# Attention scores as plain fp32 products on the two row halves of TensorE, with one maximum per unit

## The chip, the cores and the metric

The kernel runs on one core of a Trainium2 chip. The metric is device time in microseconds from the start to the end of one execution. The engines are TensorE (PE, with its weight loads shown as PEld), VectorE (DVE), ScalarE (ACT), GpSimd (POOL) and SyncE (SP), which issues the transfers.

## The reference

Attention over 4 batches and 8 heads, 576 tokens, 64 values per head, is mixed with a read of a memory and followed by two stacks of matrix products. Only the first part is touched by the change:

```python
scores = scale * np.matmul(q, k.transpose(0, 1, 3, 2))     # scale = 1/8
scores = np.where(causal, -1000000000.0, scores)
scores = scores - scores.max(-1, keepdims=True)
a = np.exp(scores)
a /= a.sum(-1, keepdims=True) + 1e-09
local = np.matmul(a, v)
...
attn = g * mem_out + (1 - g) * local
x = attn over tokens, 2304 x 512
h = (x @ w1) * (x @ w2) @ w3 ;  x = h @ w_out
h = x @ w_in ;  out = (h - tanh(h)) @ w_out2
```

All arrays are fp32, and the weights of the two stacks arrive as 64-bit numbers that the kernel decodes itself.

## The kernel before

**Stages.** The first stage, from the start to about 302 us, is the attention. In its gaps it decodes `w3` and `w_out`, multiplies them with each other (tiles `fo`, `zs`, `wf`), decodes the first tiles of `w1` and `w2` and reads the memory for the first 384 tokens. Then come the product with `w1` and `w2` and the folded weight (tiles `ab` and `x`), and from about 655 us the last stack (`h` and `o`).

**Units.** The attention works on 16 pairs of heads P. The queries of a pair are cut into five units u: units 0 to 3 have 128 queries of each head and look at 128(u+1) keys, and unit 4 has the last 64 queries of both heads together, on the two halves of the partitions, and looks at all 576 keys. That makes 80 units, which pass through seven steps in a fixed order, `ORDER = "SENTLGA"` with the lags in `LAG`: S (`scores`, then `rmax`), E (`exps`), N (`norm`), T (`trans`), L (preparation of the next pair), G (some steps of background work, `BG` per unit, from the generator `early`) and A (`av`, the product with v). A scheduler that knows only the dependences then fixes the order on each engine.

**Preparation (`load_qk`, `prep_qk`).** `load_qk` fetches q and k of a pair, transposed, with each 64-row head twice, on partitions 0 to 63 and again on 64 to 127, in two transfers of 576 KB (L196; for the first pair six smaller ones). The pool `r` has `RB` = 2 buffers. `prep_qk` makes reduced-precision parts that TensorE multiplies in one pass: ACT writes the scaled high part of q (L219), DVE overwrites partitions 64 to 127 with the low part (L224), ACT and POOL write the high part of k (`ks`, L204 and L208), and DVE and POOL the low part (L226). The 128 rows of the array thus hold the high and the low part of one head's q.

**Scores and softmax.** `scores` makes two PSUM tiles `sc` of one bank per unit from u = 2 on, one for each head (for unit 4 one for each part of the keys, 320 and 256), and one tile for both heads where they fit in a bank (u < `U1` = 2). Each head takes two matmuls, with the high and the low part of k, and one with the mask (`identb`, `maskb`). The pool of `sc` has `SB` = 4 banks. `rmax` takes the maximum on DVE (L391 for both heads at once in units 0 and 1; L394 once for each tile, with L397 joining the two of unit 4). `exps` runs on ACT, one instruction for each tile, with the sum read out after it (L407). `norm` adds 1e-9 and inverts on DVE (L416, L418, L420) and scales on POOL (L427). `trans` turns the result with TensorE (tiles `t`, L459 to L470) and copies it to `g` on ACT or DVE (`copy`). `av` multiplies v and `g` as plain fp32, the two heads on the two halves of the array's columns, into tiles `o`. The memory read (`mem_mm`, tiles `mo`) also uses plain fp32, in 64 x 64 quarters of the array.

```python
for y in range(2):                     # before: S, for each tile
    scores(n, y)
    rmax(n, y)
```

## Time and profile before

| | |
|---|---|
| median of 3 runs | 1062.58 us (1062.35 to 1063.51) |
| the profiled execution's own time | 1063.58 us |
| its span in the trace | 1061.8 us |
| PE busy in the span | 986.8 us, 93% |
| DVE busy in the span | 816.0 us, 77% |
| ACT busy in the span | 614.4 us, 58% |
| POOL busy in the span | 423.4 us, 40% |

The span runs from the first to the last instruction of the trace; the profiled execution's own time is 1.8 us longer, which lies around the span. A share of busy time is an average over stages with different limits, so it is read stage by stage. A matmul's record reaches to its modelled end, after the next one has begun, so records overlap. An fp32 product appears as two MATMUL records, an fp32r product as one. "f32" in a shape stands for both types where the operand is read by TensorE.

### The profile page before, as it was taken

Reading aid. Unit: us, or ns where it says so; the run is one execution under the profiler, and the core shown is the slowest. Engines: PE = TensorE matmul, PEld = TensorE weight load, DVE = VectorE, ACT = ScalarE, POOL = GpSimd, SP = SyncE. Lnnn points to the kernel's source line nnn. Section 1 sums busy time; section 2 is a strip of 40 time slices with the busy share of each in tenths; the row PEclk is TensorE's granted clock in tenths of the full one; section 3 lists DMA queues with packets and bytes.
Section 4 is the critical chain, followed back from the end, with each engine's and each line's share of the span. In section 5 each row is a group of like instructions: output and inputs, shape, how many; then the busy total and the mean of one; then the engine's idle time right before and its main releaser. Section 6 shows DMA issues by size and latency. Waiting matters only on the chain.

```text
span 1061.8 us, 15818 instructions
## 1 busy us (share of the span) xinstructions
PE 986.8 (93%) x5512; PEld 862.6 (81%) x5512; DVE 816.0 (77%) x1473; ACT 614.4 (58%) x1419; POOL 423.4 (40%) x432
## 2 busy tenths in 40 slices
PE   5799898978998898999999997999999999999998
PEld 3576666655687787999999997989999999999997
DVE  7989998999869998558221288788778788787776
ACT  5567677666732443334121444877777776776764
POOL 5888777777656422200000185322222222222221
PEclk9699999999999898999999999999999999999999
DMA  9764675552324454215000010000000000000000
GB/s 248 190 168 118 176 197 131 135 134 85 95 71 143 142 181 149 60 52 168 30 1 1 1 61 1 1 1 30 1 1 30 1 31 1 2 30 1 31 1 30
DMA packets 44415, 77.73 MB, mean 73 GB/s; under 512 B 5168, under 2 KB 30000, under 8 KB 42416
## 3 DMA queue, kind: packets, MB, share of 16 engines
q1 hardware_dynamic: 44336, 76.73, 25.7%
q8 instruction: 43, 0.70, 0.3%
q14 instruction: 36, 0.29, 0.1%
HBM read 72.00 MB, written 4.72 MB: 72 GB/s over the span
## 4 chain that ended last, share of the span: by engine, by line
PE 66%; DVE 21%; issue 4%; POOL 4%; ACT 2%; DMA 2%; SPq 0%; DVEq 0%; POOLq 0%; ACTq 0%
PE o L143 21%; PE h L143 19%; PE ab L143 13%; PE x L143 7%; DVE T L81 3%; DVE T L75 2%; PE sc L143 2%; POOL p L427 2%; DVE st L394 2%; DVE T L84 2%; PE fo L143 2%; DVE qs L224 2%; DVE T L77 2%; PE t L459 1%; DVE ks L226 1%
## 5 line engine op out<-in xcount | busy, mean ns | idle before, releaser
L925 POOL TENSOR_TENSOR gl<-s,gh 128x384 fp32r<-128x384 f32 x96 | 100.6, 1048 | 292.5 <-ACT gh L919 281.8
L427 POOL TENSOR_SCALAR p<-p,st 128x128 f32<-128x128 f32 (+2 forms) x144 | 111.7, 787 | 55.1 <-DVE st L420 25.8
L143 PE MATMUL x<-abh,wf 128*128 128x384 f32 x384 | 110.5, 349 | 4.1 <-ACT abh L726 4.1
L143 PE MATMUL ab<-xh,wa 128*128 128x384 f32 x384 | 110.3, 345 | 4.0 <-DVE a L723 2.0
L143 PE MATMUL ab<-xh,wb 128*128 128x384 f32 x384 | 108.4, 340 | 2.9 <-POOL wb L96 2.0
L143 PE MATMUL sc<-ks,qs 128*128 128x256 f32 (+4 forms) x384 | 91.7, 358 | 18.5 <-DVE qs L224 9.5
L407 ACT ACTIVATE p<-sc,st 128x256 f32<-128x256 f32 (+4 forms) x160 | 82.5, 527 | 32.6 <-DVE st L394 13.3
L901 DVE SCALAR_TENSOR_TENSOR s<-s,u 128x384 f32<-128x384 f32 x96 | 82.0, 855 | 22.0 <-ACT s L891 21.0
L723 DVE TENSOR_TENSOR a<-ab,a 128x384 f32<-128x384 f32 x48 | 26.4, 551 | 85.8 <-PE ab L143 73.0
L74 ACT ACTIVATE T<-raw 128x512 f32<-128x512 f32 x72 | 48.7, 677 | 67.8 <-POOL wa L99 14.0
L897 ACT ACTIVATE u<-u,pc 128x384 f32<-128x384 f32 x96 | 59.3, 619 | 43.6 <-DVE s L901 43.5
L143 PEld LDWEIGHTS sc<-ks,qs 128*128 128x128 f32 x384 | 63.0, 205 | 26.1 <-ACT p L407 10.1
L907 DVE TENSOR_TENSOR t<-h,t 128x384 f32<-128x384 f32 x96 | 53.3, 555 | 38.1 <-ACT t L890 37.7
L143 PEld LDWEIGHTS ab<-xh,wa 128*128 128x128 f32 x384 | 71.2, 191 | 8.8 <-issue 3.2
L143 PEld LDWEIGHTS x<-abh,wf 128*128 128x128 f32 x384 | 72.8, 195 | 5.3 <-ACT abh L726 5.0
L459 PE MATMUL t<-ident,p 128*128 128x128 f32 x320 | 54.7, 292 | 22.4 <-DVE g L440 8.1
L889 ACT ACTIVATE u<-h 128x384 f32<-128x384 f32 x96 | 47.0, 490 | 47.2 <-PE h L143 47.2
L143 PEld LDWEIGHTS ab<-xh,wb 128*128 128x128 f32 x384 | 71.2, 191 | 3.9 <-POOL wb L96 2.3
L143 PE MATMUL x<-abl,wf 128*128 128x384 f32 x192 | 67.9, 354 | 4.2 <-DVE abl L727 4.2
L906 DVE SCALAR_TENSOR_TENSOR s<-s,s 128x384 f32<-128x384 f32 x96 | 61.3, 638 | 8.5 <-DVE s L901 0.9
L143 PE MATMUL ab<-xl,wa 128*128 128x384 f32 x192 | 65.6, 341 | 0.0
L913 DVE COPY_PREDICATED s<-u,t 128x384 f32<-128x384 uint32 x96 | 58.5, 610 | 8.6 <-ACT t L890 0.5
(228 smaller groups left out, 2796.6 us busy)
## 6 DMA issues: line engine op xcount, KB each, us to landing
r<-in_qk SPq DMA_DIRECT2D x30, 576.0 KB, 7.4
raw<-in_wo SPq DMA_DIRECT2D x24, 512.0 KB, 3.6
raw<-in_w3t SPq DMA_DIRECT2D x16, 512.0 KB, 4.8
raw<-in_w SPq DMA_DIRECT2D x16, 512.0 KB, 3.6
raw<-in_wi SPq DMA_DIRECT2D x16, 512.0 KB, 3.8
v<-in_vt SPq DMA_DIRECT2D x16, 320.0 KB, 6.6
mw<-in_qt SPq DMA_DIRECT2D x18, 256.0 KB, 3.1
out<-ob SPq DMA_DIRECT2D x18, 256.0 KB, 2.3
```

What stands on the lines that cost most here:

```text
L74: AC.activation(out=tf, in_=hw.bitcast(F32), func=AF.Abs)
L143: return PE.matmul(o, lhsT, rhs, start=start, stop=stop).ins
L407: mark["A"][n] = AC.activation(out=p_t[n][:, o:o + w], in_=sc_t.pop((n, x))[:, 0:w], func=AF.Exp, bias=st[:, b:b + 1], accum_out=st[:, 2 + ...
L427: (DV if NV[u] == "V" else PO).tensor_scalar(out=pr, in0=pr, scalar1=sc, scalar2=1.0, op0=ALU.mult, op1=ALU.mult)
L459: PE.transpose(t[:, m], p[:, K * h + 128 * kb:K * h + 128 * kb + 128], ident)
L889: AC.activation(out=u, in_=o, func=AF.Square)
L897: AC.activation(out=u, in_=u, func=AF.Relu, bias=pc[:, 2:3])
L901: DV.scalar_tensor_tensor(out=s1, in0=s1, scalar=k2[0], in1=u, op0=ALU.add, op1=ALU.mult)
L906: DV.scalar_tensor_tensor(out=s1, in0=s2, scalar=k2[1], in1=s1, op0=ALU.add, op1=ALU.mult)
L907: DV.tensor_tensor(out=t, in0=o, in1=t, op=ALU.subtract)
L913: DV.copy_predicated(out=s1, mask=u[:].bitcast(U32), data=t)
L925: PO.tensor_tensor(out=l, in0=s1, in1=h[:].bitcast(F32), op=ALU.subtract)
```

## The change

q and k are fetched once, the first head of the pair on partitions 0 to 63 and the second on 64 to 127, in one transfer of 576 KB per pair in place of two, into one of three buffers. No parts are made; ACT scales q in place (`scale_q`), at the step L of unit 2 of the pair before. The scores are plain fp32 products with 64 rows: head 0 on the upper row half of the array, head 1 on the lower, each into its own bank of a two-bank tile. Unit 4 uses the four 64 x 64 quarters and cuts the keys into 288 and 288. `rmax` is one instruction per unit, over both banks, and unit 4 has one exponential of 576 columns instead of two. The pool of `sc` has two tiles of two banks in place of four of one. The masks, `norm` but for the sum of unit 4, `trans`, `av`, the background work and everything after the attention stay.

```diff
-    PB, RB = 5, 2
+    PB, RB = 5, 3
-    SB = 4
+    SB = 2
     def load_qk(P):
-        r = apr.tile([128, 4, 576], F32, tag="r", name="r")
-        for c in ((slice(1, 3), slice(0, 1), slice(3, 4)) if P == 0 else (slice(0, 4),)):
-            for x in (0, 64):
-                SP.dma_start(out=r[x:x + 64, c], in_=qk[P].rearrange("p (a n) -> p a n", a=4)[:, c])
+        r = qk_t[P] = apr.tile([128, 2, 576], F32, tag="r", name="r")
+        for c in (slice(0, 128), slice(128, 576)) if P == 0 else (slice(0, 576),):
+            SP.dma_start(out=r[:, :, c], in_=qk[P].rearrange("p (a n) -> p a n", a=2)[:, :, c])
-    def prep_qk(P):
...
+    def scale_q(P):
+        for c in (slice(0, 128), slice(128, 576)) if P == 0 else (slice(0, 576),):
+            q = qk_t[P][:, 0, c]
+            AC.activation(out=q, in_=q, func=AF.Copy, scale=0.125)
+        def scores(n):
             P, u = units[n]
+            q, k = qk_t[P][:, 0], qk_t[P][:, 1]
+            hr = [(h, slice(64 * h, 64 * h + 64)) for h in range(2)]
+            sc = sc_t[n] = pss.tile([128, 2, 512], F32, tag="sc", name="sc")
+            if u < 4:
+                K = 128 * (u + 1)
+                for h, r in hr:
+                    mm(sc[:, h, 0:K], q[r, 128 * u:128 * u + 128], k[r, 0:K], True, False)
+                for h, r in hr:
+                    mm(sc[:, h, K - 128:K], identb, maskb[:, 0:128], False, True)
             else:
+                for x in range(2):
+                    for h, r in hr:
+                        y = x ^ h
+                        mm(sc[r, y, 0:288], q[r, 512:576], k[r, 288 * y:288 * y + 288], True, y == 0)
+                mm(sc[:, 1, 224:288], identb, maskb[:, 128:192], False, True)
-            mark["V"][n] = DV.tensor_reduce(out=st_t[n][:, x:x + 1], in_=sc_t[n, x][:, 0:width(u, x)], axis=AX.X,
-                                            op=ALU.max, negate=True).ins
-            if u == 4 and x == 1:
-                DV.tensor_tensor(out=st_t[n][:, 0:1], in0=st_t[n][:, 0:1], in1=st_t[n][:, 1:2], op=ALU.min)
+            mark["V"][n] = DV.tensor_reduce(out=st[:, 0:2] if u < 4 else st[:, 0:1], in_=seen(n),
+                                            axis=AX.X if u < 4 else AX.XY, op=ALU.max, negate=True).ins
-            else:
-                DV.scalar_tensor_tensor(out=st[:, 4:5], in0=st[:, 2:3], scalar=1e-9, in1=st[:, 3:4],
-                                        op0=ALU.add, op1=ALU.add)
+            DV.tensor_scalar(out=st[:, 4:4 + w], in0=st[:, 2:2 + w], scalar1=1e-9, scalar2=None, op0=ALU.add)
             elif x == "L":
+                if u == 0 and 1 <= P <= 16 - RB:
+                    load_qk(P + RB - 1)
+                if u == 2 and P < 15:
+                    scale_q(P + 1)
```

The order on TensorE changes as follows. Before, in a pair in the middle of the folding (units 2 and 3; `sc` are the scores, `t` the transposes, `o` the product with v), the scores of the two heads were separate groups, with other work between them:

```order
L143 MATMUL sc<-ks_106,qs_104 128x384 x2
L143 LDWEIGHTS identb
L143 MATMUL sc<-maskb,identb 128x128
L143 MATMUL sc<-ks_106,qs_104 128x512 x2
L143 LDWEIGHTS identb
L143 MATMUL sc<-maskb,identb 128x128
L459 MATMUL t<-ident,p 128x128 x2
L143 MATMUL o<-g_790,v_109 64x256 x2
L143 MATMUL o<-g_790,v_109 64x128 x2
L143 MATMUL sc<-ks_106,qs_104 128x512 x2
L143 LDWEIGHTS identb
L143 MATMUL sc<-maskb,identb 128x128
```

In the changed kernel the same two units of a pair in the same stretch read:

```order
L143 MATMUL sc<-r 128x384 x2
L143 LDWEIGHTS identb
L143 MATMUL sc<-maskb,identb 128x128
L143 LDWEIGHTS identb
L143 MATMUL sc<-maskb,identb 128x128
L402 MATMUL t<-ident,p 128x128 x4
L406 MATMUL t<-ident,p 64x128
L143 MATMUL sc<-r 128x512 x2
L143 LDWEIGHTS identb
L143 MATMUL sc<-maskb,identb 128x128
L143 LDWEIGHTS identb
L143 MATMUL sc<-maskb,identb 128x128
```

The two heads' products now stand next to each other and the masks come after both; the other work stands between units only.

On DVE, before, in the stretch that ends shortly before an output group is copied to `xs` (`st` are the maxima and sums, `T` the decoder, `qs` and `ks` the low parts):

```order
L391 TENSOR_REDUCE st<-sc 128x2
L226 TENSOR_TENSOR ks_106<-r,ks_106 128x576
L224 SCALAR_TENSOR_TENSOR qs_104<-r,qs_104 64x576 x2
L397 TENSOR_TENSOR st<-st 128x1
L416 TENSOR_SCALAR st<-st 128x2
L75 TENSOR_SCALAR T<-T 128x512
L416 TENSOR_SCALAR st<-st 128x2
L420 RECIPROCAL st<-st 128x2
L77 TENSOR_SCALAR T<-T 128x512
```

In the changed kernel the stretch ahead of the copy of the same output group reads:

```order
L337 TENSOR_REDUCE st<-sc 128x2
L81 SCALAR_TENSOR_TENSOR T<-raw,T 128x512
L355 TENSOR_SCALAR st<-st 128x2
L84 SCALAR_TENSOR_TENSOR T<-raw,T 128x512
L356 RECIPROCAL st<-st 128x2
L355 TENSOR_SCALAR st<-st 128x2
L337 TENSOR_REDUCE st<-sc 128x2
L356 RECIPROCAL st<-st 128x2
L355 TENSOR_SCALAR st<-st 128x2
```

The three low-part instructions and the joining of two maxima are gone, and only decoder steps stand between the softmax instructions.

## Rows read from the trace of the kernel before

**Rows 1.** The page's first part: busy us, share of the span, instructions.

```profile
span 1061.8 us, 15818 instructions
PE 986.8 (93%) x5512; PEld 862.6 (81%) x5512; DVE 816.0 (77%) x1473; ACT 614.4 (58%) x1419; POOL 423.4 (40%) x432
```

**Rows 2.** Busy time by stretches: length, then each engine's, granted clock, DMA share, GB/s.

```profile
10.00:60.00 50.00, 37.23 (x180) 26.22 (x180) 45.94 (x89) 29.94 (x84) 39.24 (x40) 0.76 0.86 217
60.00:120.00 60.00, 54.59 (x373) 39.92 (x371) 54.60 (x114) 42.06 (x118) 49.42 (x55) 1.00 0.55 147
120.00:270.00 150.00, 126.53 (x847) 91.80 (x846) 146.10 (x299) 104.13 (x298) 113.59 (x124) 0.99 0.54 141
270.00:302.00 32.00, 30.53 (x212) 21.33 (x213) 23.48 (x62) 20.24 (x58) 17.21 (x25) 1.00 0.25 69
```

**Rows 3.** Groups on DVE, 0 to 302 us: busy us, mean ns, idle before.

```profile
L224 DVE SCALAR_TENSOR_TENSOR qs<-r,qs 64x576 fp32r<-64x576 f32 x32 | 30.7, 978 | 7.4 <-ACT qs L219 6.7
L226 DVE TENSOR_TENSOR ks<-r,ks 128x576 fp32r<-128x576 f32 x16 | 22.4, 1403 | 1.9 <-POOL ks L208 1.8
L394 DVE TENSOR_REDUCE st<-sc 128x1 f32<-128x512 f32 x32 | 21.6, 678 | 1.2 <-PE sc L143 1.2
...
L416 DVE TENSOR_SCALAR st<-st 128x2 f32<-128x2 f32 x64 | 17.6, 278 | 1.0 <-ACT p L407 1.0
...
L418 DVE SCALAR_TENSOR_TENSOR st<-st 128x1 f32<-128x1 f32 x16 | 8.5, 534 | 1.2 <-ACT p L407 1.1
...
L397 DVE TENSOR_TENSOR st<-st 128x1 f32<-128x1 f32 x16 | 6.6, 410 | 0.2
L394 DVE TENSOR_REDUCE st<-sc 128x1 f32<-128x256 f32 x16 | 6.5, 409 | 0.5 <-PE sc L143 0.5
```

**Rows 4.** Groups on ACT and POOL, 0 to 302 us, same columns.

```profile
L219 ACT ACTIVATE qs<-r 128x576 fp32r<-128x576 f32 x32 | 20.9, 691 | 4.4 <-DMA r<-in_qk 4.4
...
L226 POOL TENSOR_TENSOR ks<-r,ks 128x576 fp32r<-128x576 f32 x16 | 26.0, 1627 | 0.1
```

**Rows 5.** PE in order of time near 70 us: start us, length us, what, count.

```profile
69.50 0.40 PE L143 MATMUL sc<-ks,qs 128*128 128x256 f32 x2
...
70.15 0.59 PE L143 MATMUL sc<-ks,qs 128*128 128x384 f32 x2
...
71.09 0.71 PE L143 MATMUL sc<-ks,qs 128*128 128x512 f32 x2
71.65 0.23 PE L143 MATMUL sc<-maskb,identb 128*128 128x128 bf16 x1
71.71 0.39 PE L459 MATMUL t<-ident,p 128*128 128x128 f32 x2
```

**Rows 6.** PE in order of time, near 442 us and then near 64 us.

```profile
441.75 2.82 PE L143 MATMUL mo<-mq,mc 64*64 64x192 f32 x32
444.50 0.96 PE L143 MATMUL x<-abh,wf 128*128 128x384 f32 x4
...
63.22 2.16 PE L143 MATMUL o<-g,v 128*64 128x320 f32 x16
65.31 2.84 PE L143 MATMUL fo<-z,zs 128*128 128x512 f32 x11
```

**Rows 7.** PE's waits, 10 to 302 us: total us, times, longest.

```profile
PE t L459 <- DVE g L440: 8.1, 10, 2.6
...
PE sc L143 <- ACT p L407: 6.6, 13, 0.9
```

**Rows 8.** Two groups on ACT, 0 to 302 us: the exponential and its sum.

```profile
L407 ACT ACTIVATION_READ_ACCUMULATOR p<-sc,st 128x1 f32 x160 | 33.5, 210 | 0.0
...
L407 ACT ACTIVATE p<-sc,st 128x512 f32<-128x512 f32 x32 | 21.9, 694 | 2.1 <-DVE st L394 2.0
```

**Rows 9.** Start of the program in order of time: first loads, first scores.

```profile
0.74 3.76 SPq L196 DMA_DIRECT2D r<-in_qk  x6
...
7.56 1.84 PE L143 MATMUL sc<-ks,qs 128*128 128x128 f32 x6 [7.56 <-DVE qs L224]
```

More of the change, by code (lines that the diff above doesn't have):

```diff
@@ L323, in block_kernel @@
         PO.memset(pc[:, 2:3], -TANH_SPLIT ** 2)
-        for i in range(2):
-            PO.memset(QF[i][:, 0:64].bitcast(U32), 0)
-            PO.memset(QF[i][:, 1216:1280].bitcast(U32), 0)
         xs = {}
@@ new lines, in seen, with rmax, exps @@
+        def seen(n):
+            P, u = units[n]
+            return sc_t[n][:, :, 0:128 * (u + 1) if u < 4 else 288]
+        def rmax(n):
+            P, u = units[n]
+            st = st_t[n] = ap4.tile([128, 8], F32, tag="st", name="st")
+            mark["V"][n] = DV.tensor_reduce(out=st[:, 0:2] if u < 4 else st[:, 0:1], in_=seen(n),
+                                            axis=AX.X if u < 4 else AX.XY, op=ALU.max, negate=True).ins
+        def exps(n):
+            P, u = units[n]
+            st, sc = st_t[n], seen(n)
+            p = p_t[n] = ap3.tile([128, PW[u]], F32, tag=f"p{u}", name="p")
+            p = p[:].rearrange("p (a n) -> p a n", a=2)
+            for x in [slice(0, 1), slice(1, 2)] if u < 4 else [slice(0, 2)]:
+                mark["A"][n] = AC.activation(out=p[:, x], in_=sc[:, x], func=AF.Exp, bias=st[:, x.start:x.start + 1],
+                                             accum_out=st[:, 2 + x.start:3 + x.start]).ins
+            sc_t.pop(n)
@@ L626, in block_kernel @@
         NU = len(units)
-        pp = prep_qk(0)
-        next(pp)
-        next(pp)
+        scale_q(0)
         bg, bgc = early(), [0]
@@ L644, in do @@
             if x == "S":
-                if u == 0 and P >= 2:
-                    run(pp)
-                for y in range(2):
-                    scores(n, y)
-                    rmax(n, y)
+                scores(n)
+                rmax(n)
             elif x == "E":
-                for y in range(2):
-                    exps(n, y)
+                exps(n)
             elif x == "N":
@@ L661, in do @@
             elif x == "L":
-                if u == 0 and P >= 1:
-                    run(pp)
-                    pp = prep_qk(P + 1) if P + 1 < 16 else iter(())
-                for _ in range(PS):
-                    next(pp, None)
+                if u == 0 and 1 <= P <= 16 - RB:
+                    load_qk(P + RB - 1)
+                if u == 2 and P < 15:
+                    scale_q(P + 1)
             elif x == "G":
```

108 lines of the change are left out of this document (6 added, 102 removed).

## The prediction

> **What bounds the kernel now.** The page's first part names PE, 93% busy over the span [rows 1]. That is an average over stages, so I read the busy time by stretches next, and only those of the attention, since the change touches nothing behind it [rows 2]. Look at the longest stretch, 120 to 270 us: DVE is busy 146.1 of 150 us, 97%, and PE 126.5, 84%. From 10 to 302 us, 292 us in all, the four rows add up to 270.1 us for DVE, 248.9 for PE, 196.4 for ACT and 219.5 for POOL. So DVE sets the pace of this stage, PE is next with 43 us of idle time, and only the last 32 us already belong to PE (30.5 of 32). The groups on DVE then show what its time goes to [rows 3], and the timeline and waits of PE what PE can give and take [rows 5 to 7].
>
> **What DVE loses.** The low part of q goes: 32 instructions of 978 ns, 30.7 us. The low part of k on DVE goes: 16 of 1403 ns, 22.4 us. Joining the two maxima of unit 4 goes: 16 of 410 ns, 6.6 us. Unit 4's sum of two sums (534 ns) becomes an addition like that of the other units (278 ns): 16 x 0.256 = 4.1 us. The maxima of units 2, 3 and 4 become one instruction each. Of the same kind, 512 columns take 678 ns and 256 take 409 ns, so a column costs 1.05 ns and an instruction about 140 ns beside its columns; 48 instructions fewer give 6.7 us. Together 70.5 us, all [rows 3]. DVE's sum falls from 270 to about 200 us of the 292. It stops being the bound, and none of these 70 us comes through beyond the point at which another engine takes over.
>
> **What ACT and POOL lose.** ACT made q's high parts in 20.9 us and now scales q in place, 16 instructions of the same width at 691 ns, 11.1 us; its part of k's high parts goes too. POOL loses 26.0 us of k's low parts [rows 4] and its copies of k. Neither was the bound; I cost both at nothing. Both keep more slack than PE, whose load is higher.
>
> **What PE gets.** Counted in streamed columns nothing changes: before, each head took two one-pass products, now one product that the trace shows as two records. How long such products take is seen in two places [rows 6]. In the memory read 16 plain fp32 products of 192 columns, in 64 x 64 quarters, take 444.50 - 441.75 = 2.75 us. At the upper clock level, 2.4 GHz, four passes over 192 columns are 320 ns; sixteen in a row would be 5.12 us, eight pairs side by side 2.56 us. So two products on different quarters run at the same time, and the visit costs 0.19 us beside its columns. The product with v says the same for column halves: three pairs of 320 columns and one of 192, 1152 columns, are 1.92 us at four passes, and took 2.09 us. That is 1.67 ns for a column of a pair and 0.17 to 0.19 us for a visit.
>
> After the change a pair of heads needs 128 + 256 + 384 + 512 = 1280 columns in units 0 to 3 and 576 in unit 4, so 1856 x 1.67 ns = 3.10 us, plus five visits, 0.95 us, plus nine masks at the 0.06 us or less between a mask's start and the next instruction's (71.65 to 71.71), 0.5 us: 4.5 us. Before, from start to start, units 1 and 2 took 0.65 and 0.94 us, half of unit 3 took 0.62 us [rows 5]. With unit 0 taken as unit 1, and unit 4, which streams about as many columns, as unit 3, that is 0.65 + 0.65 + 0.94 + 1.24 + 1.24 = 4.7 us. PE thus gains 0.2 us per pair, 3 us in all. Row halves as such, with 128 output columns, are in no row. The bound from below is the pairs' price just used; from above each head runs alone, which doubles the 1280 columns: 16 x 2.13 = 34 us more. I take the overlap, since quarters and column halves both show it, and keep the other end as a rival.
>
> A rule of the Trainium skill speaks against the change: "FP8 and Floating Point Precision", section Matmul Precision, has true fp32 as four passes through the array, where the old products were one pass each. By that rule alone the scores would take twice as long on PE; the rows above agree with the four passes, and the two heads side by side are what pays for them. A second rule, in "TensorEngine Tiling (Array Packing)", Key Properties, says that a change of tiling mode drains the engine. The trace agrees with a price of about 0.18 us a visit, which stands in the sum.
>
> **The sum.** PE's 248.9 us become 246. A record lasts past the start of the next one: the scores at 71.09 us last 0.71 us and the mask begins after 0.56 [rows 5], so each pause of PE hides 0.15 us of drain that counts as busy. The waits are 0.5 to 0.8 us each (8.1 us over 10, 6.6 over 13 [rows 7]); 43 us of idle time are then some 65 pauses and 10 us of drain, of which I let 7 go with closer packing: 239 us. An engine that sets the pace was 97% busy here when it was DVE, and PE was 95% busy in its own last stretch and 91% from 60 to 120 us [rows 2]; I take 93%. The 292 us become 239 / 0.93 = 257, a gain of 35 us.
>
> The start adds a little. The first loads are six transfers, 3.76 us of issue on the SP queue, and the first scores start at 7.56 us behind two DVE instructions [rows 9]. Now two transfers stand ahead of the mask and identity, and DVE does nothing before the first maximum. I give 3 us, between 0 and 5. Half the bytes of q and k go as well; the first 50 us moved 217 GB/s with DMA 86% busy and the clock at 0.76 [rows 2], so this stretch may gain more than its share: 2 us. In all 40 us: 1063.6 - 40 = **1023 us** for an execution like the profiled one, which stood 1.0 us above the median of the runs shown, so the median would be 1022 to 1023.
>
> **Rivals.**
>
> *The gain is larger.* PE's demand shrinks more as drains and mask stalls merge, and the next bound is DVE with 200 us: at 97% that is 206 us, a gain of 86 as the outer end. PE cannot be under its streamed work, for which 225 us at 95% is a generous case: 237 us, gain 55 + 5, so 1003 us. For it: one group of scores per unit instead of two to four, with other work between. Against it: transposes wait for POOL and copies, whatever DVE does.
>
> *The two score tiles become the wait.* There were four banks, freed head by head; now two tiles, freed when both exponentials are done. For unit 3 a tile is held for about 1.1 us of matmuls, a maximum of 1024 columns (140 + 1024 x 1.05 = 1.2 us [rows 3]) and two exponentials with their sums (2 x (694 + 210) ns = 1.8 us [rows 8]), 4.1 us, so 2.1 us per unit with two tiles, less for the others: 8 us for a pair of heads against the (302 - 10) / 16 = 18 us that a pair takes now. It decides only where queueing behind decoder steps doubles each hold. PE already waited for an exponential 13 times, 6.6 us [rows 7]. If PE's share then rises from 85% (248.9 of 292) to 87% only, with few pauses merged, the stage is 243 / 0.87 = 279 us: gain 13 + 3, 1047 us.
>
> *Slower: the row halves don't overlap.* With 128 output columns the two heads share all columns of the array, which neither row shows. Then PE needs 34 us more, 280 us, and with today's packing of about 90% the stage takes 311 us: 19 us more than 292, less 3 at the start, 1080 us; with 97% it takes 289 us and comes out even. It decides at once: the second head's record would start one pass behind the first.
>
> *No change:* what the DVE sheds is taken by waits for POOL, ACT and transfers in the same order of work, within 0.2% (2 us, about what a measurement of this kernel can tell from no change).
>
> **How the numbers follow.** Forecast (1012 to 1035 us) 0.60; the larger gain (995 to 1012) 0.13; the score tiles (1035 to 1055) 0.15; row halves apart 0.09, of which 0.03 still comes out faster; no change 0.03. Faster: 0.60 + 0.13 + 0.15 + 0.03 = 0.91; same 0.03; slower 0.06. The range takes the forecast, most of the larger gain and the nearer half of the tiles' case: 1002 to 1045 us.
>
> **What would show it.** Right: the attention ends near 262 us, DVE busy about 200 us in it, PE over 90% of each stretch; the two heads' score records start within 0.01 us of each other, 512 columns take 0.43 us a record pair; nothing changes behind the attention. Wrong: records of the two heads one behind the other; PE idle over 15% with waits of scores for exponentials (the tiles); the attention's end at 302 us with all engines under 85%.

## The result and the profile after

The changed kernel takes 1036.74 us in the median (1034.81 to 1039.02, four runs), against 1062.46 us for the kernel before, measured beside it: a ratio of 0.976 (95% interval 0.973 to 0.978), so it is 25.7 us faster. The forecast was 1023 us, with 1002 to 1045 as its range. The time lies in the range, and the gain is about a third smaller than forecast. The profiled execution took 1034.81 us, 28.8 us less than the profiled one of before, and its span is 28.8 us shorter too.

The first part of the page of the changed kernel answers to [rows 1]:

```profile
span 1033.0 us, 15587 instructions
PE 984.2 (95%) x5512; PEld 826.1 (80%) x5512; DVE 745.9 (72%) x1361; ACT 594.7 (58%) x1356; POOL 361.8 (35%) x396
```

DVE lost 70.1 us of busy time over the span, PE only 2.6. The difference lies in the attention, so the busy time by stretches is read next. The attention ends with the last product with v: at 304.2 us before, at 278.0 us now, 26.1 us earlier; the other 2.6 us came behind it. First the whole attention of the kernel before, which [rows 2] shows in pieces (columns as there: length, PE, PEld, DVE, ACT, POOL, granted clock, DMA share, GB/s):

```profile
10.00:304.40 294.40, 251.27 (x1628) 180.62 (x1628) 270.11 (x560) 196.54 (x556) 219.51 (x242) 0.95 0.56 146
```

The same view of the changed kernel, in pieces and whole:

```profile
10.00:60.00 50.00, 42.80 (x253) 23.56 (x254) 39.26 (x87) 33.59 (x95) 30.68 (x41) 1.00 0.50 171
60.00:120.00 60.00, 59.21 (x387) 34.87 (x386) 44.53 (x95) 41.92 (x115) 38.00 (x54) 1.00 0.41 129
120.00:240.00 120.00, 111.88 (x727) 66.10 (x726) 96.00 (x213) 79.95 (x224) 74.61 (x95) 0.99 0.40 128
240.00:270.00 30.00, 28.59 (x207) 16.67 (x206) 19.53 (x50) 21.26 (x59) 14.57 (x23) 1.00 0.21 64
10.00:278.30 268.30, 250.78 (x1622) 147.29 (x1623) 202.31 (x448) 178.21 (x494) 159.91 (x211) 0.99 0.39 126
```

The last row says nearly everything. DVE fell from 270.1 to 202.3 us, so its sum no longer sets the pace. PE's busy time did not fall at all, 251.3 to 250.8. What fell is PE's idle time, the length less the busy time: 294.4 - 251.3 = 43.1 us before, 268.3 - 250.8 = 17.5 us now. PE is busy 93.5% of the attention, 85% before. Nearly all of the gain in this stage, 25.6 of 26.1 us, is PE's idle time.

DVE's maxima after, which answer to the L394 and L397 groups in [rows 3], are one instruction a unit over both banks (busy us, mean ns, then the idle time before):

```profile
L337 DVE TENSOR_REDUCE st<-sc 128x2 f32<-128x1024 f32 x16 | 19.4, 1213 | 0.0
...
L337 DVE TENSOR_REDUCE st<-sc 128x2 f32<-128x768 f32 x16 | 15.2, 948 | 3.7 <-PE sc L143 3.7
L337 DVE TENSOR_REDUCE st<-sc 128x1 f32<-128x576 f32 x16 | 12.0, 751 | 11.7 <-PE sc L143 11.7
```

Two banks of 512 columns cost 1213 ns, where two instructions of 678 ns stood. DVE now waits for PE's scores, which it did little of before.

PE in order of time, in a pair in the middle of the folding (start, length, what, count), shows how the pairs of heads run:

```profile
140.37 0.92 PE L143 MATMUL sc<-r 64*128 64x384 f32 x4
141.22 0.28 PE L143 MATMUL sc<-maskb,identb 128*128 128x128 bf16 x2
...
144.61 0.27 PE L406 MATMUL t<-ident,p 128*64 128x128 f32 x1
144.81 1.13 PE L143 MATMUL sc<-r 64*128 64x512 f32 x4
145.87 0.28 PE L143 MATMUL sc<-maskb,identb 128*128 128x128 bf16 x2
146.00 0.39 PE L395 MATMUL t<-ident,p 128*128 128x128 f32 x2
```

Four records of 512 columns, two for each head, stand between 144.81 and 145.87: 1.06 us for what both heads need. The records of the two heads start 0.007 us apart. So the row halves do run at the same time, with 128 output columns too.

In this part I also count PE from start to start: from a matmul's start to the next one's, but no longer than its own record less 0.16 us, the part of a record that lasts on when nothing follows it (its drain). So this count leaves drains out. It is my own count over all records, made the same way for every kernel from its start to the attention's end. The scores took 74.0 us by it before and take 65.0 now, the masks 8.3 and 8.8.

### The profile page after: what moved, and what is told of

Same layout as the page of the kernel before. It is cut to its first block, busy times and chain, and to the rows that moved or that the text cites. A ratio compares the mean times of both kernels' runs of the same rounds, so it can differ in the third digit from the quotient of the medians.

```text
span 1033.0 us, 15587 instructions
## 1 busy us (share of the span) xinstructions
PE 984.2 (95%) x5512; PEld 826.1 (80%) x5512; DVE 745.9 (72%) x1361; ACT 594.7 (58%) x1356; POOL 361.8 (35%) x396
## 4 chain that ended last, share of the span: by engine, by line
PE 79%; DVE 11%; issue 3%; DMA 3%; ACT 2%; POOL 2%; SPq 0%; DVEq 0%; ACTq 0%; POOLq 0%
PE o L143 24%; PE h L143 20%; PE ab L143 14%; PE x L143 7%; PE sc L143 6%; PE fo L143 4%; PE t L395 3%; DVE T L81 2%; DVE T L75 2%; DVE st L337 1%; PE mo L143 1%; DVE T L77 1%; ACT p L346 1%; DMA raw<-in_wi 1%; DVE T L84 1%
## 5 line engine op out<-in xcount | busy, mean ns | idle before, releaser
L363 POOL TENSOR_SCALAR p<-p,st 128x128 f32<-128x128 f32 (+2 forms) x144 | 94.5, 669 | 63.4 <-DVE st L356 32.3
L143 PE MATMUL sc<-r 64*64 64x288 f32 (+4 forms) x384 | 79.6, 480 | 17.5 <-ACT p L346 11.7
L346 ACT ACTIVATE p<-sc,st 128x128 f32<-128x128 f32 (+2 forms) x144 | 78.3, 549 | 29.8 <-DVE st L337 25.1
L647 DVE TENSOR_TENSOR a<-ab,a 128x384 f32<-128x384 f32 x48 | 26.4, 551 | 86.3 <-PE ab L143 73.5
L74 ACT ACTIVATE T<-raw 128x512 f32<-128x512 f32 x72 | 48.6, 674 | 62.3 <-DMA raw<-in_wi 11.9
L337 DVE TENSOR_REDUCE st<-sc 128x2 f32<-128x256 f32 (+4 forms) x80 | 64.1, 803 | 26.6 <-PE sc L143 26.2
L143 PE MATMUL ab<-xl,wb 128*128 128x384 f32 x192 | 64.7, 337 | 0.0
```

The costliest lines, as they stand in the source:

```text
L74: AC.activation(out=tf, in_=hw.bitcast(F32), func=AF.Abs)
L143: return PE.matmul(o, lhsT, rhs, start=start, stop=stop).ins
L337: mark["V"][n] = DV.tensor_reduce(out=st[:, 0:2] if u < 4 else st[:, 0:1], in_=seen(n), axis=AX.X if u < 4 else AX.XY, op=ALU.max, negate= ...
L346: mark["A"][n] = AC.activation(out=p[:, x], in_=sc[:, x], func=AF.Exp, bias=st[:, x.start:x.start + 1], accum_out=st[:, 2 + x.start:3 + x. ...
L363: (DV if NV[u] == "V" else PO).tensor_scalar(out=pr, in0=pr, scalar1=sc, scalar2=1.0, op0=ALU.mult, op1=ALU.mult)
```

## The experiments

One table holds all runs. Ratio is to the kernel before, measured beside each run. End is where the windows row of the attention ends (it begins at 10 us); PE idle is its length less PE's busy time; scores is my start-to-start count of the score products. The columns from end on are of the one profiled execution, which in three runs lies off the median: e4's took 1058.56 us, e8's 1040.92 and e10's 1073.83.

| kernel | median us | ratio (95%) | end us | PE busy | PE idle | DVE busy | scores |
|---|---|---|---|---|---|---|---|
| before | 1062.46 | 1 | 304.4 | 251.3 | 43.1 | 270.1 | 74.0 |
| after | 1036.74 | 0.976 (0.973 to 0.978) | 278.3 | 250.8 | 17.5 | 202.3 | 65.0 |
| no low parts (e1) | 1045.06 | 0.984 (0.981 to 0.988) | 286.5 | 248.8 | 27.7 | 239.0 | 74.5 |
| vector work back (e2) | 1052.4 | 0.990 (0.988 to 0.993) | 293.0 | 256.5 | 26.6 | 231.1 | 67.7 |
| one pass (e3) | 1009.65 | 0.950 (0.948 to 0.952) | 247.1 | 211.6 | 25.5 | 205.9 | 15.9 |
| four score tiles (e4) | 1066.31 | 1.002 (0.999 to 1.005) | 300.5 | 285.4 | 5.1 | 212.3 | 93.3 |
| two maxima (e5) | 1039.6 | 0.977 (0.975 to 0.980) | 279.7 | 252.0 | 17.7 | 206.2 | 65.9 |
| shared tile (e6) | 1047.51 | 0.985 (0.983 to 0.988) | 291.0 | 254.3 | 26.7 | 209.9 | 63.9 |
| no masks (e7) | 1034.84 | 0.973 (0.971 to 0.975) | 278.1 | 247.0 | 21.1 | 211.4 | 66.7 |
| loads twice (e8) | 1037.48 | 0.976 (0.973 to 0.978) | 280.2 | 253.0 | 17.2 | 204.6 | 65.8 |
| no maximum (e9) | 1040.17 | 0.979 (0.978 to 0.981) | 281.8 | 256.9 | 14.9 | 163.9 | 70.5 |
| heads apart (e10) | 1078.25 | 1.015 (1.012 to 1.017) | 316.1 | 300.0 | 6.1 | 205.9 | 107.8 |
| all paired (e11) | 1062.43 | 1.000 (0.998 to 1.002) | 303.5 | 260.9 | 32.6 | 212.0 | 62.3 |
| rounded, one pass (e12) | 1015.85 | 0.956 (0.954 to 0.958) | 256.9 | 225.5 | 21.4 | 209.9 | 35.5 |

### e1: only the low parts leave the kernel before

```diff
 def prep_qk(P):
...
-            DV.scalar_tensor_tensor(out=q[64:128, d], in0=rq[64:128, d], scalar=0.125,
...
+            if P < 2:
+                DV.scalar_tensor_tensor(out=q[64:128, d], in0=rq[64:128, d], scalar=0.125,
...
+            if P < 2 or (KLE if P else K0)[n] != "V":
+                (DV if (KLE if P else K0)[n] == "V" else PO).tensor_tensor(out=kl[:, c], in0=rk[:, c], in1=kh[:, c].bitcast(F32),
...
```

> The kernel before, with VectorE's low parts (32 of q, 16 of k) made for the first two pairs of heads only; the other pairs multiply the parts that were left in the two buffers, so their scores lack the right low parts. GpSimd's low parts, all matmuls, tiles, loads and maxima stay. Removed from VectorE: 28 x 0.978 + 14 x 1.403 = 47 us, so 270 becomes 223 us in the attention. Theory A (the change gains because VectorE's work goes and TensorE, about 250 us busy at 93%, becomes the bound): the attention ends near 276 us and the kernel near 1036 to 1042 us, with nothing else of the change. Theory C (half the bytes of q and k, three buffers or the single maximum bring the gain): 1055 us or more.

Measured: 1045.06 us, 17.5 us less than the kernel before (1062.59 beside it). That is between the two theories, nearer to A, whose attention would have ended at 276 us. The windows row:

```profile
10.00:286.50 276.50, 248.76 (x1628) 180.76 (x1628) 239.02 (x518) 196.14 (x556) 200.93 (x242) 0.95 0.61 156
```

Here PE does exactly what it did, with 74.5 us of scores, and yet its idle time falls from 43.1 to 27.7 us. So two thirds of the gain of the change, 17.5 of 25.7 us, is had by taking instructions off DVE and nothing else, though DVE's busy time fell by only 31 of the 68 us. It did not fall by the 47 us of the instructions that are gone, because others took longer: the additions of `norm` last 369 ns each instead of 278. POOL, with the same 242 instructions, is busy 18.6 us less (its scalings of p take 679 ns instead of 787), so the run doesn't tell DVE's own queue from what DVE's work does to POOL. The other 8 us need the rest of the change.

### e2: 31 us of work put back on DVE

```diff
+    if u in (1, 3):                   # step L, into a tile nobody reads
+        DV.scalar_tensor_tensor(out=scr[64:128], in0=r[64:128, 0], scalar=0.125,
+                                in1=r[64:128, 1], op0=ALU.mult, op1=ALU.subtract)
```

> The changed kernel with 32 instructions of the size of the old low part of q put back on VectorE, two per pair of heads, into a tile that nobody reads: 31 us more VectorE work, 203 becomes 234 us of about 279. Theory A: VectorE has that much slack behind TensorE, so 0 to 8 us slower than the changed kernel, 1037 to 1045 us. Theory B (what bounds it now is the chain through VectorE's queue, scores to maximum to exponential with two score tiles): each added instruction lengthens the hold of a tile, 15 us slower or more, 1052 us and up.

Measured: 1052.4 us, 15.7 us slower than the changed kernel. That is the price of theory B (15 us or more) and twice the most that theory A gave (8), although DVE with 231.1 us of 283 does not set the pace. The waits show where it comes from. The changed kernel first (who waits for whom: total us, times, longest):

```profile
POOL p L363 <- DVE st L356: 32.3, 20, 3.1
DVE st L337 <- PE sc L143: 26.2, 25, 4.8
ACT p L346 <- DVE st L337: 25.1, 30, 2.6
...
PE sc L143 <- ACT p L346: 11.7, 13, 4.5
```

And with the work back:

```profile
ACT p L347 <- DVE st L338: 48.5, 39, 4.8
```

The exponential's wait for the maximum doubles, from 25.1 to 48.5 us. An instruction of about 1 us that stands ahead of a maximum in DVE's queue delays the maximum, that the exponential, and that the return of a score tile to PE: the score products' weight loads wait 23.5 us for exponentials instead of 16.4, the products themselves 13.3 instead of 11.7. POOL's scalings of p got longer too, 714 ns instead of 669, and this run can't tell the two apart. PE's idle time rises by 9.1 us, and its busy time by 5.7; 12 records of units 0 to 3 lost their partner, of which e4 tells more. DVE is no bound by its sum, but its queue lies on the chain from scores to exponential. Both theories thus hold a part: e3 shows theory A's.

### e3: scores in one pass

```diff
-            AC.activation(out=q, in_=q, func=AF.Copy, scale=0.125)
+            rr = one_t.setdefault(P, None) or aprr.tile([128, 2, 576], BF16, tag="rr", name="rr")
+            one_t[P] = rr
+            AC.activation(out=rr[:, 0, c], in_=q, func=AF.Copy, scale=0.125)
+            AC.activation(out=rr[:, 1, c], in_=qk_t[P][:, 1, c], func=AF.Copy)
```

> The changed kernel with q and k rounded to bf16 by ScalarE, so that a score product is one pass and one record instead of four passes and two: scores are less precise. TensorE loses three quarters of 3.1 us of columns per pair of heads, 37 us in all, and the second record's weight load; ScalarE gains 11 us for k. Theory A (TensorE bounds the attention): 20 to 30 us faster than the changed kernel, 1007 to 1017 us. Theory B (two score tiles): a tile's hold falls from 4.1 to about 3.4 us in the largest unit, 5 to 10 us faster at most.

Measured: 1009.65 us, 27.1 us less than the changed kernel, in theory A's range, with DVE's work as it was:

```profile
10.00:247.10 237.10, 211.63 (x1434) 134.05 (x1434) 205.88 (x448) 181.85 (x508) 166.01 (x211) 0.97 0.43 141
```

PE's busy time fell by 39.2 us, 31.2 us of which reached the attention's end. This settles what sets the pace of the changed kernel: not DVE's sum, whose 206 us fit into 237 with room to spare, but PE. The scores went from 65.0 to 15.9 us, about a quarter. The rule of the Trainium skill that the forecast weighed ("FP8 and Floating Point Precision", Matmul Precision: true fp32 takes four passes) agrees with that ratio.

### e4: four score tiles of one bank

```diff
-    SB = 2
+    SB = 4
-            sc = sc_t[n] = pss.tile([128, 2, 512], F32, tag="sc", name="sc")
+            sc = sc_t[n] = [pss.tile([128, 512], F32, tag="sc", name="sc") for _ in range(2)]
...
+            for h, t in enumerate(seen(n)):
+                mark["V"][n] = DV.tensor_reduce(out=st[:, h:h + 1], in_=t, axis=AX.X, op=ALU.max, negate=True).ins
```

> The changed kernel with the scores of each head in a tile of one bank, four tiles, a maximum per head (and the minimum and sum of two for unit 4), and an exponential per bank also in unit 4: products as in the change, tiles and maxima as before. VectorE gets 48 maxima x 0.14 us and 16 joinings back, 18 us with the slower sum; ScalarE 16 exponentials. Theory A: within 5 us of the changed kernel. Theory B: a bank is free after its own exponential, so TensorE's waits for exponentials (11.7 us and 16.4 us before weight loads) go, 8 us or more faster.

Measured: 1066.31 us over ten runs, which neither theory had: the whole gain is gone. The runs fall in two groups, three from 1056.6 to 1058.68 us and seven from 1065.79 to 1069.27, and the profiled one (1058.56) is of the lower; what parts them isn't known. In it the gain is not lost by waiting, since PE's idle time is the smallest of all, 5.1 us. PE's busy time is 34.6 us higher. The row, and PE's timeline, say where it lies:

```profile
10.00:300.50 290.50, 285.37 (x1622) 162.01 (x1623) 212.31 (x544) 183.85 (x526) 160.16 (x211) 0.99 0.37 116
```

```profile
151.57 0.91 PE L143 MATMUL sc<-r 64*128 64x384 f32 x2
152.41 0.23 PE L143 MATMUL sc<-maskb,identb 128*128 128x128 bf16 x1
152.57 0.91 PE L143 MATMUL sc<-r 64*128 64x384 f32 x2
153.41 0.23 PE L143 MATMUL sc<-maskb,identb 128*128 128x128 bf16 x1
```

With a tile for each head the scheduler no longer keeps the two heads' products next to each other: one head's two records run, then its mask, then the other head's. From start to mask that is 0.84 us for one head (151.57 to 152.41). The pair above took 0.85 us for both (140.37 to 141.22). A row half that runs alone costs what two cost together. Of 64 records at each width, 60 ran without a partner at 128 columns, 32 at 256, 44 at 384 and 48 at 512; in the changed kernel none did (40 of the 128 records of unit 4 did).

### e5: two maxima per unit

```diff
-            mark["V"][n] = DV.tensor_reduce(out=st[:, 0:2] ..., in_=seen(n), ...)
+            for h in range(2 if u < 4 else 1):
+                mark["V"][n] = DV.tensor_reduce(out=st[:, h:h + 1] ..., in_=seen(n)[:, h] ..., ...)
```

> The changed kernel with one maximum per head in units 0 to 3, as two instructions on the halves of the same two-bank tile; the products stay side by side. VectorE gets 64 instructions of 0.14 us back, 9 us, and the first head's exponential may start earlier. By the run with single-bank tiles, which lost 28 us on TensorE because the two heads' products came apart: if the pairing alone made that loss, this run is 0 to 6 us slower than the changed kernel (9 us of VectorE at the half price that 31 us of it cost). If the single maximum made the gain, it is 15 us slower or more.

Measured: 1039.6 us, against 1036.74; the intervals of the two ratios (0.975 to 0.980, 0.973 to 0.978) overlap. "One maximum for both heads at once" is worth some 3 us, not clearly told from nothing. DVE's busy time rises by 3.9 us; the records of the maxima, which can overlap with others, add up to 8.8 us more, the 9 us expected.

### e6: units 0 and 1 in one score tile

```diff
+            if u == 1:
+                sc = sc_t[n] = sc_t[n - 1, "t"][:, :, 128:384]
+            else:
+                sc = sc_t[n] = pss.tile([128, 2, 512], F32, tag="sc", name="sc")
```

(Unit 1's products are ordered behind unit 0's last mask, a second difference.)

> The changed kernel with units 0 and 1 of a pair in one tile (columns 0 to 128 and 128 to 384 of each bank), so four tiles per pair of heads are needed instead of five, and TensorE can be one unit further ahead. If waits for score tiles cost time (TensorE waited 11.7 us for exponentials, weight loads 16.4), 5 to 12 us faster than the changed kernel. If TensorE's own work sets the pace, 0 to 3 us, since no product goes away.

Measured: 1047.51 us, 10.8 us slower, a miss. PE needs what it needed (scores 63.9 us), but is idle 9.2 us more, and exponentials wait longer for maxima than the 25.1 us of the changed kernel:

```profile
ACT p L354 <- DVE st L345: 36.3, 29, 3.4
```

The number of units a tile serves is not what counts. That the shared tile is given back later, after the last of four exponentials, would explain it, and so might the ordering; no run isolates either.

### e7: no masks

```diff
-                    mm(sc[:, h, 0:K], ..., True, False)
-                for h, r in hr:
-                    mm(sc[:, h, K - 128:K], identb, maskb[:, 0:128], False, True)
+                    mm(sc[:, h, 0:K], ..., True, True)
```

> The changed kernel without the 144 mask products, so the scores are not causal. TensorE loses 9 us of mask records by their start-to-start times and part of the way out of the row-half mode. TensorE bounds the attention: 8 to 14 us faster than the changed kernel. VectorE's queue or score tiles bound it: 0 to 4 us faster.

Measured: 1034.84 us; the ratio's interval overlaps that of the changed kernel, so nothing clear of the noise was gained. It is the outcome that the expectation gave to VectorE's queue or the score tiles, not the 8 us or more of a bound on TensorE's work. The masks' 8.8 us are gone, but PE's busy time fell by only 3.8, and idle time rose by 3.6:

```profile
10.00:278.10 268.10, 247.03 (x1479) 145.42 (x1478) 211.37 (x444) 176.52 (x490) 162.29 (x210) 0.97 0.39 126
```

By the start-to-start count the transposes took 50.9 us instead of 46.2, the products with v 49.6 instead of 47.5 and the scores 66.7 instead of 65.0, together 8.5 us. Most of that is the clock: its mean is 0.97 instead of 0.99, and PE's first records keep twice their later length until about 28 us instead of 22. Where the trace grants 1.00, a record of the products with v counts 102.5 ns (102.1 in the changed kernel) and one of the scores 161.1 (160.7); only the transposes are dearer, 119 against 113 ns, some 2 us. 40 of the 256 records of units 0 to 3 lost their partner. So the run says little on what a mask costs, and why PE's idle time rose isn't shown.

### e8: the loads of q and k twice

```diff
+        d = aprd.tile([128, 2, 576], F32, tag="d", name="d")
+        SP.dma_start(out=d, in_=qk[P].rearrange("p (a n) -> p a n", a=2))
```

> The changed kernel with each pair's q and k fetched a second time, into a tile that nobody reads: the bytes of the kernel before. The run before the change without low parts stood 8 us above the changed kernel, with the DMA queues 89% busy from 10 to 60 us against 50%. If half the bytes bring that part of the gain: 5 to 9 us slower than the changed kernel, lost before 60 us. If not: 0 to 2 us.

Measured: 1037.48 us, a ratio of 0.976 like the changed kernel's. DMA engines were busy 48% of the attention instead of 39%, 159 GB/s instead of 126, and nothing moved by more than the runs scatter. The halved bytes are worth nothing here.

### e9: no maximum at all

```diff
-            mark["V"][n] = DV.tensor_reduce(out=st[:, 0:2] ..., op=ALU.max, negate=True).ins
-                mark["A"][n] = AC.activation(out=p[:, x], in_=sc[:, x], func=AF.Exp, bias=st[:, x.start:x.start + 1],
+                mark["A"][n] = AC.activation(out=p[:, x], in_=sc[:, x], func=AF.Exp, bias=pc[:, 3:4],
```

> The changed kernel without maxima: the exponentials start from a bias of zero as soon as the scores stand (the softmax is the same as long as no exponential overflows, which holds for these inputs and not for any). VectorE loses 64 us, 203 becomes 139, and the way from scores to exponential no longer passes its queue. TensorE's products and their order by pairs stay. If TensorE's own work sets the pace and only its own gaps remain: 0 to 10 us faster than the changed kernel. If the chain through VectorE still causes most of TensorE's 48 us without a new product: 20 us faster or more, with TensorE's wait for exponentials (11.7 us) gone.

(The background work, which the changed kernel orders behind a unit's maximum and exponential, then stands behind the exponential alone.)

Measured: 1040.17 us, 3.4 us above the changed kernel, with intervals that overlap a little. The expectation had it faster in either case, by 0 to 10 or by 20 us, since DVE lost another 38 us of busy time and each exponential can start as soon as its scores are there:

```profile
10.00:281.80 271.80, 256.94 (x1622) 149.73 (x1623) 163.92 (x369) 177.01 (x494) 159.68 (x211) 0.98 0.39 124
```

PE's idle time did fall, by 2.6 us to 14.9; its busy time rose by 6.2. The timeline shows a torn pair:

```profile
144.58 1.12 PE L143 MATMUL sc<-r 64*128 64x512 f32 x2
145.63 0.66 PE L393 MATMUL t<-ident,p 128*128 128x128 f32 x4
146.22 1.12 PE L143 MATMUL sc<-r 64*128 64x512 f32 x2
```

One head's 512 columns run, four transpositions, then the other head's: 1.05 us twice, where the pair took 1.06 once. 36 of the 64 records of 512 columns had no partner, while in unit 4 only 4 had none, against 40; the scores took 5.5 us more. So the maxima in front of the exponentials account for little of PE's idle time in the changed kernel, and what the shorter chain gives is lost to the order that the scheduler then picks.

### e10: the two heads kept apart

```diff
-                    mm(sc[:, h, 0:K], q[r, 128 * u:128 * u + 128], k[r, 0:K], True, False)
-                for h, r in hr:
-                    mm(sc[:, h, K - 128:K], identb, maskb[:, 0:128], False, True)
+                    with tc.issue_after(sc_l[0]) if h else ExitStack():
+                        mm(sc[:, h, 0:K], q[r, 128 * u:128 * u + 128], k[r, 0:K], True, False)
+                    sc_l[0] = mm(sc[:, h, K - 128:K], identb, maskb[:, 0:128], False, True)
```

> The changed kernel with one edit on TensorE: in units 0 to 3 the second head's product is queued behind the first head's mask product, which uses all rows, so that the two row halves never run at the same time; tiles, maxima, exponentials and loads stay. By the run with single-bank tiles, a lone product takes as long as a pair, so TensorE needs 16 x 2.13 = 34 us more for columns and 64 more changes of mode at about 0.1 us: 25 to 42 us slower than the changed kernel, which would lose the whole gain. If single-bank tiles and separate maxima made that run slow: 0 to 8 us slower.

Measured: 1078.25 us, 41.5 us slower than the changed kernel and slower than the kernel before. Every record of units 0 to 3 is alone, the scores take 107.8 us instead of 65.0, and PE, busy 98% of the attention, carries that into the time almost whole:

```profile
10.00:316.10 306.10, 300.03 (x1624) 167.58 (x1624) 205.88 (x447) 180.70 (x494) 158.44 (x211) 1.00 0.35 111
```

This is what the changed kernel would be if the two heads' products were not neighbours in PE's order. Of the 49.2 us of added busy time, the scores by start to start are 42.8, so their overlap is worth more than the whole gain; drains at the further changes of mode add 12 us, and fewer pauses take some back.

### e11: unit 4 paired too

```diff
+                with tc.issue_after(t_l[n - 2]):          # unit 4's products as one group
+                    ...
+                with tc.issue_after(sc_l[0]) if u == 3 else ExitStack():
+                    trans(n)
```

> The changed kernel with an order on TensorE that keeps unit 4's four products together: they are queued behind the transposes of unit 2, and the transposes of unit 3 behind them. In the changed kernel 40 of unit 4's 128 records ran without a partner; a record that runs alone takes 0.29 us, as a pair does, so 20 pairs are bought back at 0.29 us each, 6 us of TensorE. If TensorE's own work sets the pace: 3 to 7 us faster than the changed kernel. If the forced order makes TensorE wait for transposes' inputs instead: no change or slower.

Measured: 1062.43 us over twelve runs (1057.67 to 1066.84), 25.7 us slower than the changed kernel, a miss. Every record now has its partner and the scores fell to 62.3 us, as meant. But PE's idle time rose to 32.6 us, and its busy time to 260.9 with all but the same matmuls (1636 records against 1622). In the longest stretch:

```profile
120.00:270.00 150.00, 131.53 (x816) 77.86 (x812) 110.63 (x232) 89.63 (x247) 78.56 (x104) 0.93 0.37 114
```

PE is busy 88% there, and the granted clock is 0.93 on average, between its levels of 1.2 and 2.4 GHz, where the changed kernel had 0.99 between 120 and 240 us. The lowest value in this stretch, in pieces of 10 us, came behind a piece in which PE was busy 5.99 us:

```profile
240.00:250.00 10.00, 5.99 (x39) 3.16 (x38) 9.72 (x21) 6.63 (x20) 6.39 (x8) 0.93 0.51 164
250.00:260.00 10.00, 8.96 (x53) 4.84 (x53) 6.45 (x13) 3.66 (x10) 5.59 (x7) 0.73 0.44 139
```

The exponentials' wait for maxima is 54.6 us instead of 25.1. Two ordering edges per pair are enough to lose everything: 2.7 us of matmul time were bought with 15 us of idle time and a lower clock. Which of the two edges does it was not tried.

### e12: one pass for units 0 to 3 in fp32r

```diff
+            rr = one_t.setdefault(P, None) or aprr.tile([128, 2, 576], F32R, tag="rr", name="rr")
+            one_t[P] = rr
+            AC.activation(out=rr[:, 0, c], in_=q, func=AF.Copy, scale=0.125)
+            AC.activation(out=rr[:, 1, c], in_=qk_t[P][:, 1, c], func=AF.Copy)
...
+            q, k = (one_t if u < 4 else qk_t)[P][:, 0], (one_t if u < 4 else qk_t)[P][:, 1]
```

> The changed kernel with q and k of units 0 to 3 rounded to fp32r by ScalarE and multiplied in one pass, unit 4 as plain fp32: finer rounding than bf16, and no low parts, so scores are less exact than in both kernels. TensorE loses three quarters of 16 x 2.13 us of columns, 26 us, and 128 second records with their switch; ScalarE gains 11 us. If TensorE sets the pace and fp32r runs on row halves side by side as fp32 does: 18 to 28 us faster than the changed kernel, near the run with bf16. If fp32r's weight loads are not hidden: 10 us faster or less.

Measured: 1015.85 us. Units 0 to 3 take 18.1 us of scores instead of 44.1, and PE's busy time falls by 25.3 us; 21.4 us reach the attention's end. It is the second fastest of all, after e3. Of the runs that compute the scores as plain fp32, none is clearly faster than the changed kernel.

## Why the prediction was right or wrong

**What bounds the kernel: right.** DVE set the pace before, PE does now. e1 shows the first half (17.5 us from DVE's instructions, with PE's work untouched), e3 and e10 the second (PE's work up or down moves the time, DVE's standing still). e2 adds what the forecast left to a rival, the score tiles: DVE's queue still costs time behind PE.

**DVE's 70.5 us: right in the sum.** 67.8 us in the attention, 70.1 over the span. The terms don't come through one for one, since records overlap and change their length with what runs beside them: in e1, 47 us of instructions gone were 31 us of busy time, in e9, 64.2 us of maxima were 38. So some of the agreement is luck. e5 tested one term: its 64 further maxima are 8.8 us by their records, near the 140 ns each of the forecast, 3.9 us of busy time, and some 3 us in the median.

**ACT and POOL at nothing: right for their sums**, 178.2 and 159.9 us of 268.3. What the step left out is that they stand in a chain with DVE. e2, e6 and e11 all lose time with every engine busy less than 91% of the attention, and in each the exponentials' wait for maxima is the row that grew most.

**The price of a pair of row halves: right.** 1.67 ns a column and 0.19 us a visit give 0.855 + 0.19 = 1.05 us for 512 columns; 1.06 us was measured. From the first product's start to what follows, units 0 to 3 take 0.42, 0.63, 0.85 and 1.06 us wherever the clock is at 2.4 GHz, 0.21 us beside the columns.

**What PE gains by it: wrong, and this is the step that failed.** By the count without drains the scores and masks gained more than forecast: (74.0 + 8.3) / 16 = 5.1 us per pair of heads before, (65.0 + 8.8) / 16 = 4.6 now, 8.5 us in all instead of 3. But the forecast's 4.7 and 4.5 us are times from start to start with the drains in them. So I also count PE's busy time as it stands, record by record up to the next start, leave out the drain ahead of a pause, and add the drain of other work ahead of a score product: 83.8 us before and 88.4 now, 5.2 and 5.5 us per pair, the first pair at the lower clock in both. The change thus costs PE 4.6 us where it was to give 3. The visit's 0.19 us came from the first product's start to the next instruction's, so it holds the drain on the way out and not the one on the way in, where the record ahead runs out first. The transposition at 144.61 is followed by the scores after 0.20 us, while a transposition takes 0.115 us from start to start on average (46.2 us for 400). That is 0.09 us a visit, 6.3 us in the stage, and it was put at nothing. Unit 4, whose records lost their partner in part, adds 2.7 us (20.9 us, 18.2 in e11). The rule of the Trainium skill in "TensorEngine Tiling (Array Packing)", Key Properties, that a change of mode drains the engine, agrees in kind, in both directions; the page gives no price for it.

**PE's busy time of 239 us: wrong by that step.** The forecast took 246 us for the products and let 7 of 10 us of drain go "with closer packing". Measured: 250.8. The part of the busy time that is drain, busy less start-to-start from 10 us on, was 251.3 - 234.0 = 17.3 us before and is 250.8 - 224.4 = 26.4 now. Read by what comes behind each record, the drain ahead of pauses did fall, from 8.8 us (55 pauses, close to the forecast's 65 and 10 us) to 4.3 (27), by 4.5 instead of 7. The drain on the way into and out of the scores rose from 1.2 to 14.4 us, 0.09 us at each of 167 places; the rest stood at 7.3 and 7.7. e4 and e10, with 259 and 299 such places, have 23.6 and 26.4 us there. No run removes these drains alone, so this stays a count over records.

**The share of 93%: right**, 93.5%, though the stretch from 10 to 60 us has 86% where over 90% was to be seen in each. With the measured busy time the forecast's own last line is 250.8 / 0.93 = 270 us, against 268.3 measured; with 239 it was 257. The books: of the 40 us forecast for the profiled execution 28.8 came. The stage gave 26.1 instead of 35, the start and the bytes nothing instead of 5, and 2.6 came behind the attention: 8.9 + 5 - 2.6 = 11.3 us less, which is the miss.

**The start's 3 us: wrong.** The first scores start at 3.79 us instead of 7.56, as said. But the lead is gone within the first pair (timeline of all engines, then of PE alone):

```profile
3.79 0.80 PE L143 MATMUL sc<-r 64*128 64x128 f32 x4 [3.79 <-ACT r L194]
...
6.57 1.23 PE L143 MATMUL sc<-r 64*128 64x256 f32 x4 [1.98 <-ACT r L194]
...
7.72 0.61 PE L143 MATMUL sc<-maskb,identb 128*128 128x128 bf16 x4
...
10.73 0.43 DVE L75 TENSOR_SCALAR T<-T 128x512 f32<-128x512 f32 x1 [0.82 <-ACT T L74]
11.07 1.01 DVE L337 TENSOR_REDUCE st<-sc 128x2 f32<-128x256 f32 x2
...
12.81 1.65 PE L143 MATMUL sc<-r 64*128 64x384 f32 x4 [4.49 <-ACT p L346]
...
14.72 2.08 PE L143 MATMUL sc<-r 64*128 64x512 f32 x4
```

Both score tiles are full after two units. Their maxima could start behind the masks, near 8.3 us, but stand on DVE behind short instructions on the gates, which wait for a transfer until 8.92 us, and behind a decoder step that waits for ACT, which waits for another; they start at 11.07. The third unit waits 4.49 us for the exponentials behind them, and unit 3 starts at 14.72 us, where the kernel before started it at 13.03. The forecast counted the start of the first product and not the way of its tile back to PE.

**The 2 us for half the bytes: wrong.** e8 moves the bytes again and loses nothing. The stretch from 10 to 60 us did gain more than its share, PE being busy 42.80 us against 37.23, but the rows point to the clock. Before:

```profile
20.00:30.00 10.00, 5.08 (x22) 3.01 (x22) 9.81 (x14) 5.84 (x13) 10.00 (x9) 0.58 1.01 249
30.00:40.00 10.00, 6.60 (x31) 4.90 (x33) 9.70 (x13) 2.54 (x8) 7.07 (x7) 0.57 0.90 202
```

And the changed kernel:

```profile
20.00:30.00 10.00, 7.34 (x47) 3.74 (x45) 9.90 (x19) 5.88 (x16) 7.96 (x9) 1.00 0.35 114
30.00:40.00 10.00, 10.00 (x69) 5.60 (x69) 7.86 (x19) 8.19 (x25) 7.33 (x11) 1.00 0.52 166
```

Before, PE was mostly at 1.2 GHz for these 20 us, in which it was busy 5.08 and 6.60 of 10 us, after 8.48 of 10 from 10 to 20 us; now it is at 2.4 GHz from about 22 us on. e1, which keeps the bytes and sheds DVE work, stood between, with PE busy 36.94 us and a clock of 0.86 from 10 to 60 us. This can be part of the 8 us that lie between e1 and the changed kernel; no run isolates it.

**The rivals.** *The row halves don't overlap* was put at 1080 us; they do overlap, and e10, which takes it away, measured 1078.25. So its mechanism holds where the order parts the heads: the two products must be neighbours. That the two times agree is luck, since the rival had 280 us of PE's work at 90% and e10 has 300 at 98%. *The score tiles become the wait* came true in part: the wait of scores for exponentials is now PE's largest, 11.7 us against 6.6 before [rows 7]. Of it 4.49 us lie at the start, 1.7 of them ahead of 10 us, so it is about 10 of the 17.5 us that PE is idle in the row. Four tiles are not the remedy (e4), since they tear the pairs apart. *The larger gain* needs less matmul work, as e3 and e12 have, not better packing. *No change* fell.

**Behind the attention** nothing was to change; 2.6 us less came there, which I leave unexplained.

## What to carry to other kernels

Taking work from the busiest engine pays until the next one is full, so cost the change on that next one, and count its drains with its columns: here a change between the whole array and its row halves cost 0.09 us on the way in and again on the way out. Two products on two row halves cost what one costs, but only while they are next to each other in TensorE's order; give them a common tile or another reason to stay together, and look in the trace for records without a partner. An engine at 80% may still delay others when a long instruction stands in its queue ahead of a short one that others wait for.

## What the runs showed of the hardware that was not expected

A plain fp32 product on one row half takes the same time alone as two do side by side: 0.84 us alone and 0.85 for the pair at 384 columns, 1.05 and 1.06 at 512. Running heads apart cost 42 us over 16 pairs of heads, with the drains of the further changes of mode in it.

TensorE can be 98% busy in this stage, with the transposes, copies and softmax around it as they are: e4 and e10 leave it 5.1 and 6.1 us idle of 290 and 306, in a stage that is 22 and 38 us longer. In the changed kernel it is 93.5%.

The very first products run at the lower level, though a row of their stretch gives 1.00: in the changed kernel the four records of 512 columns at 14.72 us last 2.08 us and those at 144.81 last 1.13. The trace holds no clock record before 21.9 us (18.2 us in the kernel before), and a row counts such time as 1.00, so the level there is read from the records' lengths.

Small changes of order are worth as much as the whole change: e4, e9 and e11 have the matrix products of the changed kernel and lie 30, 3 (not clear of the noise) and 26 us above it, and e4 and e11 also spread over 13 and 9 us between their ten and twelve runs, against 4 us over four for the changed kernel. Why the forced order of e11 costs so much is not settled.
